# A new emission order and PSUM pools from tables, in a kernel of linear attention and an MLP

## The chip, the core and the metric

One core of a Trainium2 chip. The metric is the device time of one execution, in microseconds (us). Engines are called by the profile's names: PE is the TensorE matmul, PEld its weight load, DVE VectorE, ACT ScalarE, POOL GpSimd, SP the engine whose queue issues the DMAs.

## The reference

Attention with random features, then an MLP, all in float32. Batch 8, 8 heads, 576 tokens, head width 64, 128 features; the MLP has 4608 tokens, model width 512, inner width 2048.

```python
q_s, k_s = q * scale, k * scale                  # scale = 64 ** -0.25
def phi(x):
    h = einsum('bhsd,md->bhsm', x, omega) - sum(x * x) / 2
    return exp(h - max(h)) / sqrt(m)
kv = einsum('bhsm,bhsd->bhmd', phi(k_s), v);  z = sum(phi(k_s), axis=2)
attn = einsum(phi(q_s), kv) / (einsum(phi(q_s), z) + 1e-6)
x = attn as (4608, 512);  h = x @ w_in
out = (h * sigmoid(h)) @ w_out
```

## The kernel before, in words

**Windows.** Attention works in 32 windows, one for each batch and pair of heads. A window n goes through a chain over all engines: SP loads q, k and v (raw, nat, v). PE projects them on omega (proj for k and for q; mid or mids for the middle block; in windows 18 to 31 one proj unit does k and q). DVE takes the row maxima (top, nb). ACT does the exp (exp in strips of four blocks of columns, or DVE subtracts and ACT does expall). POOL adds the columns of phi(k) (sums, esl; ACT does esh between them). PE spreads that sum to all rows (z, line 664). DVE computes the denominators against it (den, line 696). POOL multiplies phi(q) by their reciprocals (norm, line 707; DVE in three windows). PE transposes the result in three triples (turn, line 713), ACT copies each out of PSUM (en, line 717). PE computes phi(k) times v (kv, line 672), ACT copies it (kt), PE transposes it (ktt, line 680), ACT copies it (kw), and PE multiplies for the numerator (num, line 734). From window 2 on, kv of window n + 1 and num of window n are one unit, kvnum. ACT copies the result (xh), and for the first 12 windows DVE makes a low half (xl). In windows 0 to 7 the squares are done by ACT on the raw input (r2, line 546).

**The MLP.** Four windows are one tile of 512 tokens. Every float32 operand is split into a high and a low part, so that each product is three fp32r matmuls of 128x512 (`thrice`, line 905). Tile 0 runs stage 1 (units s1, three matmuls each) and stage 2 (s2) in full. Its weights are taken from the input, rounded and split by ACT (re, wh), DVE (wd) and POOL (wlo). Tiles 1 to 8 go by pairs with seven products of sums of quarters in place of eight: tiles 1 and 2 run stage 1 in full, then `pr` units (six matmuls) for stage 2; the later pairs run `deep` units for stage 1, too. ACT applies Silu (silu, sA, si) and makes high parts (hi, ohi), DVE makes differences and low parts (dif, lo, xd, olo).

**The order of the work.** All this is registered as 3716 units in `Plan` (line 122): 933 for PE, 863 for ACT, 960 for DVE, 423 for POOL, 537 for SP. A unit has an engine, a duration in the plan, a function that emits its instructions, the units it needs, the ring buffers it takes and frees, and the number of PSUM banks it takes. `Plan.run` (line 139) is a list scheduler in the kernel's Python code: at each step it takes, over the engines, the ready unit that could start first by its own durations, ties within 0.25 us going to the lower number in the table `RANK` (line 282). Line 1546 then emits the units in that order. Each engine's queue runs its instructions in the order in which they are emitted, so the order of an engine is fixed when the kernel is built. In this kernel the numbers in `RANK` are the places, 0 to 3715, in which the scheduler issues the units: it reproduces its table unit for unit.

**PSUM.** There are eight banks in three pools: acc (4) for stage 2 and the sums of products, h (2) for stage 1 of tiles 0 to 2, att (2). A bank that an attention unit takes comes from the pool that `bank_pools` (inside `Plan.run`, line 171) chooses: always att, and h or acc too in stretches in which its rules allow it. A unit waits for the last reader of the buffer that it is given. ACT must load another function table (`ACT_TABLE_LOAD`) whenever it changes between exp and Silu.

Of the kernel before, what the change touches and what calls it, by code (L numbers as in the profile page):

```python
# [21 lines left out]
NPAIR = H // 2  # L22
# [12 lines left out]
LAG = 2  # L35
# [40 lines left out]
SWITCH = 1.3  # L76
HANDOFF = {"PE": 0.3, "ACT": 0.25, "DVE": 0.22, "POOL": 0.2, "SP": 0.2}
CALM = 0.5
TURN = 0.14
# [36 lines left out]
def tiled_by(u):  # L116
    if u["name"][0] == "proj" and u["name"][1] in FOLD:
        return None
    return {"proj": "rows", "kv": "columns", "num": "columns", "kvnum": "columns"}.get(u["name"][0])


class Plan:
# [16 lines left out]
    def run(self):  # L139
        assert len(RANK) == len(self.units)  # L140
        rank = dict(zip(self.units, RANK))
        end, first = {}, {}
        slots = {r: [] for r in RINGS}
        pipe = port = 0.0
        holds = []
        free_at = {e: 0.0 for e in ("PE", "ACT", "DVE", "POOL", "SP")}
        table = mode = None
        order = []
        children, missing = {}, {}
        ready = {e: [] for e in free_at}  # L150
        for n, u in self.units.items():
            missing[n] = len(u["after"]) + len(u["order"])
            for a in u["after"] + u["order"]:
                children.setdefault(a, []).append(n)
            if not missing[n]:
                ready[u["eng"]].append(u)

        freed = {r: [] for r in RINGS}
        home, frees, users = {}, {}, {}
        for x, names in self.freed_by.items():  # L160
            users[x] = len(names)
            for n in names:
                frees.setdefault(n, []).append(x)

        def slot_time(ring, back=0):
            i = len(slots[ring]) + back - RINGS[ring]
            if i < 0:
                return 0.0
            return freed[ring][i] if i < len(freed[ring]) else None

        def bank_pools(u):
            pools = ["att"]
            if u["key"] > mm_time(START[2] + MIX):
                pools.append("h")
            if u["key"] < mm_time(24 * LAG) - 1 or (
                LEND[0] < u["key"] < LEND[1] and slots["acc"] and slots["acc"][-1][0] != "ch"
            ):
                pools.append("acc")
            if u["key"] < START_MLP - 1:
                pools.append("h")  # L180
            chosen, when, used = [], 0.0, {p: 0 for p in pools}
            for _ in range(u["banks"]):
                best = None
                for p in pools:
                    t = slot_time(p, used[p])
                    if t is not None and (best is None or t < best[0]):
                        best = (t, p)
                if best is None:
                    return None, None
                used[best[1]] += 1  # L190
                chosen.append(best[1])
                when = max(when, best[0])
            return chosen, when

        while any(ready.values()):
            best = None
            for e, us in ready.items():
                pick, least = None, None
                for u in us:
                    t = 0.0  # L200
                    for a in u["after"]:
                        if self.units[a]["eng"] == e and not self.units[a]["lat"]:
                            t = max(t, end[a])
                        else:
                            t = max(t, first[a] + (CALM if e == "PE" and t > START_MLP else 0.0))
                    ok, taken = True, []
                    for ring, _ in u["alloc"]:
                        s = slot_time(ring, taken.count(ring))
                        taken.append(ring)
                        if s is None:  # L210
                            ok = False
                            break
                        t = max(t, s)
                    pools = ()
                    if ok and u["banks"]:
                        pools, s = bank_pools(u)
                        ok = pools is not None
                        if ok:
                            t = max(t, s)
                    if not ok:  # L220
                        continue
                    t = max(t, free_at[e])
                    if u["port"] and e == "POOL":
                        t = max(t, port)
                    elif u["port"]:
                        for a, b in holds:
                            if a <= t < b:
                                t = b
                    key = rank[u["name"]]
                    least = t if least is None else min(least, t)  # L230
                    pick = (pick or []) + [(u, pools, key, t)]
                if not pick:
                    continue
                p = min((p for p in pick if p[3] <= least + 0.25), key=lambda p: p[2:])
                if best is None or p[3] < best[3]:
                    best = p
            assert best is not None, [u["name"] for us in ready.values() for u in us][:40]
            u, pools, _, t = best
            e, n = u["eng"], u["name"]
            ready[e].remove(u)  # L240
            dur = u["dur"]
            if u["table"] and u["table"] != table:
                dur += SWITCH
                table = u["table"]
            if e == "PE":
                if tiled_by(u) != mode:
                    dur += TURN
                mode = tiled_by(u)
            u["cost"] = dur
            free_at[e] = t + dur  # L250
            if u["port"] and e == "POOL":
                n_ = int(u["port"])
                holds = holds[-12:] + [(t + dur * i / n_, t + dur * (i + 1) / n_ - 0.05) for i in range(n_)]
            elif u["port"]:
                port = t + dur
            done = t + dur
            if u["lat"]:
                pipe = max(pipe, t + dur + 1.0) + u["lat"]
                done = max(pipe, t + dur + 2.2) + LANDING
            end[n] = done  # L260
            first[n] = done + HANDOFF[e]
            for ring, i in u["alloc"]:
                slots[ring].append(i)
                home[i] = ring
            for j, p in enumerate(pools):
                slots[p].append(("bank", n, j))
                home["bank", n, j] = p
            for x in frees.get(n, ()):
                users[x] -= 1
                if not users[x]:  # L270
                    freed[home[x]].append(max(end[a] + HANDOFF[self.units[a]["eng"]] for a in self.freed_by[x]))
# [1336 lines left out]
```

## Time and profile before

| | |
|---|---|
| median of 3 runs | 982.38 us (982.08 to 982.41) |
| the profiled execution's own time | 978.92 us |
| its span, first to last instruction | 977.1 us |
| mean granted TensorE clock | 0.994 |
| busy PE / DVE / ACT / POOL | 948.6 / 764.9 / 646.5 / 402.7 us |

The span is what the profile's rows divide up. The profiled execution is 3.46 us shorter than the median of the runs; its own time lies 1.8 us over the span. The busy time of PE counts overlapping matmuls once, and a stall of a fraction of a matmul inside a stream does not show as idle.

### The profile page before, as it was taken

How to read it: one execution, taken by the hardware profiler on the slowest of the kernel's cores; microseconds unless marked ns; L12 is line 12 of the kernel's file. 1: busy time of each engine (PE TensorE's matmuls, PEld its weight loads, DVE VectorE, ACT ScalarE, POOL GpSimd, SP SyncE). 2: the span in 40 equal slices, each digit the busy share in tenths (PEclk: the TensorE clock that was granted, in tenths of full speed). 3: DMA queues.
4: the chain of work that ended last, by engine and by line, in shares of the span. 5: the costliest groups of instructions: out<-in, count | busy, mean ns of one | idle time of the engine just before them, and what ended most of it. 6: DMA issues, size and time to landing. Idle time of an engine off the chain costs nothing.

```text
span 977.1 us, 16378 instructions
## 1 busy us (share of the span) xinstructions
PE 948.6 (97%) x5558; PEld 767.2 (79%) x5558; DVE 764.9 (78%) x1610; ACT 646.5 (66%) x1233; POOL 402.7 (41%) x430
## 2 busy tenths in 40 slices
PE   7879999999999999997999999999999999999998
PEld 6667887787787778785778888778888887888886
DVE  4778998588764988757999999669799966369954
ACT  8999787687987675697478766665384544235442
POOL 3666555868775858547631444222012220000000
PEclk9899999999999999999999999999999999999999
DMA  8388997999987698886676666676554556556562
GB/s 240 112 273 286 311 363 268 328 371 307 307 299 267 223 336 301 301 285 229 215 274 223 206 239 222 216 241 206 182 194 174 185 205 226 192 189 221 192 214 103
DMA packets 102708, 237.61 MB, mean 243 GB/s; under 512 B 13664, under 2 KB 44512, under 8 KB 102624
## 3 DMA queue, kind: packets, MB, share of 16 engines
q1 hardware_dynamic: 102480, 236.49, 71.3%
q8 instruction: 45, 0.74, 0.3%
q14 instruction: 39, 0.32, 0.1%
q10 hardware_dynamic: 144, 0.07, 0.0%
HBM read 192.48 MB, written 44.04 MB: 242 GB/s over the span
## 4 chain that ended last, share of the span: by engine, by line
PE 80%; ACT 9%; DVE 8%; issue 1%; DMA 1%; POOL 0%; DVEq 0%; ACTq 0%; POOLq 0%
PE ps_acc L905 56%; PE ps_h L905 9%; PE ps_att L558 3%; PE ps_att L672 2%; ACT hk L613 2%; PE ps_att L713 2%; PE ps_h L558 1%; ACT hq L613 1%; ACT in L546 1%; PE ps_att L734 1%; DVE prod L696 1%; PE ps_h L734 1%; PE ps_h L713 1%; ACT g L787 1%; DVE g L997 1%
## 5 line engine op out<-in xcount | busy, mean ns | idle before, releaser
L905 PE MATMUL ps_acc<-ts,w 128*128 128x512 f32 x2544 | 612.1, 394 | 4.3 <-ACT ts L916 1.4
L905 PEld LDWEIGHTS ps_acc<-ts,w 128*128 128x128 f32 x2544 | 469.1, 188 | 104.2 <-ACT ts L916 1.9
L947 ACT CAST ts<-g 128x1024 fp32r<-128x1024 f32 x112 | 118.0, 1055 | 118.5 <-PE ps_acc L905 114.5
L951 DVE TENSOR_TENSOR ts<-g,ts 128x1024 fp32r<-128x1024 f32 x112 | 143.7, 1287 | 33.1 <-ACT ts L947 32.9
L905 PE MATMUL ps_h<-xq,w 128*128 128x512 f32 x576 | 149.6, 400 | 0.1
L707 POOL TENSOR_TENSOR hq<-hq,rd 128x384 f32<-128x384 f32 x87 | 90.3, 1060 | 93.9 <-DVE rd L702 84.2
L905 PEld LDWEIGHTS ps_h<-xq,w 128*128 128x128 f32 x576 | 103.8, 188 | 21.6 <-DVE xq L760 0.4
L997 DVE TENSOR_TENSOR g<-ps_acc,g 128x512 f32<-128x512 f32 x144 | 95.6, 685 | 26.0 <-PE ps_acc L905 24.8
L642 POOL TENSOR_TENSOR t<-hk 128x256 f32<-128x256 f32 x64 | 55.4, 882 | 121.2 <-ACT hk L634 62.7
L943 DVE TENSOR_TENSOR g<-g,g 128x1024 f32<-128x1024 f32 x64 | 88.1, 1390 | 5.1 <-ACT g L938 4.6
L819 POOL TENSOR_TENSOR w<-g,w 128x512 fp32r<-128x512 f32 x32 | 44.9, 1417 | 31.9 <-ACT w L815 15.7
L655 POOL TENSOR_TENSOR es<-t,es 128x256 fp32r<-128x256 f32 x32 | 28.2, 882 | 60.9 <-ACT es L651 60.8
L1001 ACT ACTIVATE g<-g 128x1024 f32<-128x1024 f32 x36 | 37.7, 1059 | 22.9 <-DVE g L997 22.8
L696 DVE CUSTOM_DVE_ANT_0 prod<-hq,ps_att 128x128 f32<-128x128 f32 (+1 forms) x150 | 42.9, 286 | 11.6 <-PE ps_att L664 6.8
L542 DVE TENSOR_REDUCE sq<-in 128x9 f32<-128x576 f32 x48 | 34.8, 744 | 20.0 <-ACT in L537 19.5
L647 POOL TENSOR_TENSOR t<-t,hk 64x128 f32<-64x128 f32 x64 | 37.4, 584 | 23.7 <-ACT hk L613 20.0
L963 ACT CAST ts<-xq 128x1024 fp32r<-128x1024 f32 x21 | 22.2, 1057 | 37.2 <-PE ps_acc L905 36.8
L967 DVE TENSOR_TENSOR ts<-xq,ts 128x1024 fp32r<-128x1024 f32 x21 | 26.1, 1244 | 22.2 <-ACT ts L963 22.2
L696 DVE CUSTOM_DVE_ANT_0 prod<-hq,ps_h 128x128 f32<-128x128 f32 (+1 forms) x120 | 34.3, 286 | 6.1 <-PE ps_h L664 1.9
L1024 DVE TENSOR_TENSOR c<-ps_acc,c 128x512 f32<-128x512 f32 x48 | 30.8, 682 | 7.6 <-PE ps_acc L905 7.6
L862 POOL TENSOR_TENSOR ic<-ic 128x512 f32<-128x512 f32 x16 | 24.3, 1519 | 28.2 <-DMA ic<-w_d 15.9
L613 ACT ACTIVATE hk<-ps_att,nbk 128x128 f32<-128x128 f32 x117 | 33.9, 397 | 2.6 <-DVE nbk L592 2.2
(172 smaller groups left out, 1443.0 us busy)
## 6 DMA issues: line engine op xcount, KB each, us to landing
w<-w_d SPq DMA_DIRECT2D x168, 512.0 KB, 4.2
w<-ws_d SPq DMA_DIRECT2D x48, 512.0 KB, 4.0
v<-v SPq DMA_DIRECT2D x32, 320.0 KB, 5.0
out<-c SPq DMA_DIRECT2D x17, 512.0 KB, 4.4
in<-kT SPq DMA_DIRECT2D x24, 352.0 KB, 3.9
in<-qT SPq DMA_DIRECT2D x24, 352.0 KB, 5.3
g<-w_in SPq DMA_DIRECT2D x16, 512.0 KB, 5.1
g<-w_out SPq DMA_DIRECT2D x16, 512.0 KB, 6.0
```

Of the source, the lines that this page charges most:

```text
L558: nc.tensor.matmul(ps[:, cols], T["raw", n, who][r, o : o + P], oms[r], start=True, stop=True)
L613: nc.scalar.activation(h[:, c], ps[:, i * M : (i + 1) * M], AF.Exp, bias=bias_of(n, who, c), scale=-1.0 if n in FOLD else 1.0)
L642: nc.gpsimd.tensor_tensor(t[:, i], e[:, 5 * i : 5 * i + 2], e[:, 5 * i + 2 : 5 * i + 4], ALU.add)
L696: nc.vector.tensor_tensor_reduce(out=prod[r], in0=e[r, c], in1=z[r, j * M : (j + 1) * M], scale=1.0, scalar=GUARD, op0=ALU.mult, op1=ALU.a ...
L707: nc.gpsimd.tensor_tensor(e[:, c], e[:, c], rd[:, c].unsqueeze(2).broadcast_to([P, 3, M]), ALU.mult)
L819: nc.gpsimd.tensor_tensor(lo, T["w", i], hi.bitcast(F32), ALU.subtract)
L905: nc.tensor.matmul(ps, w(a), x[:, b], start=first and n == 0, stop=last and n == 2, **more)
L943: nc.vector.tensor_tensor(out, a, b, ALU.subtract)
L947: nc.scalar.copy(g[:, 0], T["g", p, SOURCE[j], u])
L951: nc.vector.tensor_tensor(g[:, 1], T["g", p, SOURCE[j], u], g[:, 0].bitcast(F32), ALU.subtract)
L997: nc.vector.tensor_tensor(to, T["q", p, chain, i], T["g", p, r, i // 2][:, i % 2], ALU.add)
L1001: nc.scalar.activation(g, g, AF.Silu)
```

## The change

The scheduler goes. The kernel emits the units sorted by a new table `RANK` of the same length, and the pool of each attention bank is read from a string `HOMES`, one letter for each of the 395 banks. Units, functions, instructions, ring sizes and dependencies are the same. The durations in the `add` calls change too, and two tables MODES and CHANGE are added, but nothing in the emitted program depends on them any more.

```diff
     def run(self):
         assert len(RANK) == len(self.units)
-        rank = dict(zip(self.units, RANK))
...
-        def bank_pools(u):
-            pools = ["att"]
-            if u["key"] > mm_time(START[2] + MIX):
-                pools.append("h")
...
-                p = min((p for p in pick if p[3] <= least + 0.25), key=lambda p: p[2:])
...
-        return order
+        order = sorted(zip(RANK, self.units.values()), key=lambda x: x[0])
+        homes, done = iter(HOMES), set()
+        for _, u in order:
+            assert done.issuperset(u["after"]) and done.issuperset(u["order"]), u["name"]
+            done.add(u["name"])
+            u["pools"] = [{"a": "att", "c": "acc", "h": "h"}[next(homes)] for _ in range(u["banks"])]
+        return [u for _, u in order]
 
 RANK = (
-    0, 1, 13, 2, 11, 15, 17, 19, 22, 23, 3, 14, 18, 25, 29, 30, 27, 24, 33, 31, 37, 42, 49, 6, 40, 41, 43, 47, 48, 51,
...
+)
+HOMES = (
+    "achacchaaccchcchcaacchahcacchaahcccachchccachhcchhachhacchacaahcacaccaahhahaaaaahahahaaahahaaahaahaa"
...
-        add(zn, "PE", 0.24, at(n, 7, 32), lambda ps, n=n: zsum(n, ps), after=[("esl", n)] + e["q"], banks=1,
+        add(zn, "PE", 0.233, at(n, 7, 32), lambda ps, n=n: zsum(n, ps), after=[("esl", n)] + e["q"], banks=1,
...
```

Counted from the two tables, the least number of units that must be moved to turn one order into the other: PE 272, ACT 468, DVE 433, POOL 124, SP 228. The banks of attention come from att, h and acc 213, 115 and 67 times before, 154, 129 and 112 times after; 204 of the 395 differ. "PE work" between two places of PE's order is, in what follows, the sum of the shortest spacings of the units between them in the trace (0.68 us for an s1 or s2 unit, 1.36 for pr and deep, 2.2 for kvnum, 1.9 for a proj of both, 1.7 for a proj of windows 0 to 7, 0.24 for a turn).

PE's order of the opening, from the proj of window 3 (a number alone is a window; [s1 x4] stands for four s1 units):

```
before: proj3k num0 z1 proj2q mid2q mid3k turn1 turn1 z2 turn1 proj3q kvnum1 mid3q proj4k ktt2 turn2 turn2 mid4k
        turn2 [s1 x2] z3 proj4q mid4q kvnum2 turn3 ktt3 turn3 proj5k mid5k [s1] turn3 kvnum3 proj5q ktt4 z4 mid5q
        [s1 x5] [s2 x3] turn4 [s1 x4] proj6k [s2 x4] ...
after:  proj3k z1 turn0 turn0 turn0 ktt0 proj2q mid2q ktt1 num0 turn1 mid3k turn1 z2 turn1 proj3q mid3q kvnum1
        proj4k mid4k turn2 ktt2 z3 turn2 turn2 proj4q kvnum2 mid4q proj5k mid5k turn3 turn3 turn3 ktt3 proj5q
        kvnum3 z4 [s1 x3] mid5q [s1] ktt4 [s1 x4] proj6k [s1 x3] turn4 [s1] [s2 x4] ...
```

Ahead of its first Silu, ACT had r2 of window 6 (q) and 7 (k), two re passes, kw of window 4 and the last strip of exp of window 5 (q); after the change these stand behind it, and the short xh copy of window 2 stands ahead.

PE's order around the proj of window 20 (D is a deep unit):

```
before: D kvnum17 turn18 x3 ktt18 proj20 D D D mids20 z19 kvnum18 ktt19 turn19 x3 z20 kvnum19 ktt20 proj21 D D
after:  D z18 kvnum17 D proj20 D turn18 x3 mids20 z19 D ktt18 D kvnum18 turn19 ktt19 turn19 x2 z20 kvnum19 D proj21
        ktt20 D D
```

The z unit of window 19 takes a bank of pool h in both. Before, it is the one that the second q strip of exp of window 20 frees; after, the one that a k strip of the same window frees.

## Rows read from the trace of the kernel before

**Rows 1.** Stretches: length; busy (count) of PE, PEld, DVE, ACT, POOL; clock; DMA; GB/s.
```profile
10.20:34.00 23.80, 19.17 (x172) 16.85 (x171) 15.01 (x61) 22.66 (x69) 13.20 (x20) 1.00 0.59 177
34.00:41.00 7.00, 4.88 (x21) 4.28 (x22) 5.35 (x20) 6.90 (x18) 6.62 (x9) 0.51 0.49 130
41.00:72.00 31.00, 26.78 (x216) 21.39 (x214) 25.29 (x84) 30.61 (x80) 20.07 (x25) 1.00 0.76 241
...
250.00:436.00 186.00, 185.94 (x1141) 148.82 (x1141) 136.05 (x281) 141.47 (x296) 125.02 (x120) 1.00 0.84 287
436.00:484.00 48.00, 42.05 (x305) 32.08 (x305) 38.14 (x103) 31.27 (x84) 32.96 (x38) 0.96 0.63 214
```

**Rows 2.** Timeline of ACT, 57 to 72 us (start, length, instruction, [idle before]).
```profile
57.56 1.16 ACT L546 ACTIVATE in<-in 64x1152 f32<-64x1152 f32 x1
...
63.70 1.36 ACT L787 ACTIVATE g<-g 128x512 f32<-128x512 f32 x2
...
66.53 0.68 ACT L787 ACTIVATE g<-g 128x512 f32<-128x512 f32 x1 [0.20 <-DMA g<-w_out]
...
68.83 1.13 ACT L613 ACTIVATE hq<-ps_att,nbq 128x128 f32<-128x128 f32 x4
69.98 1.28 ACT L916 ACT_TABLE_LOAD   x1
71.27 0.60 ACT L916 ACTIVATE ts<-ps_h 128x512 fp32r<-128x512 f32 x1
```

**Rows 3.** Timeline of PE in the opening.
```profile
35.79 0.90 PE L713 MATMUL ps_acc<-ident,hq 128*128 128x128 f32 x3 [3.94 <-POOL hq L707]
...
71.92 0.50 PE L905 MATMUL ps_acc<-ts,w 128*128 128x512 f32 x1 [1.44 <-ACT ts L916]
73.13 2.13 PE L905 MATMUL ps_acc<-ts,w 128*128 128x512 f32 x8 [0.71 <-DVE ts L921]
75.11 0.49 PE L713 MATMUL ps_att<-ident,hq 128*128 128x128 f32 x3
75.35 3.00 PE L905 MATMUL ps_h<-xq,w 128*128 128x512 f32 x12
78.19 1.95 PE L554 MATMUL ps_att<-omn,in 128*128 128x128 f32 x16
```

**Rows 4.** Timeline of PE, 439 to 468 us.
```profile
439.17 1.31 PE L672 MATMUL ps_att<-hk,v 128*64 128x128 f32 x20
...
441.38 0.55 PE L713 MATMUL ps_h<-ident,hq 128*128 128x128 f32 x3
441.77 0.49 PE L713 MATMUL ps_att<-ident,hq 128*128 128x128 f32 x3
...
453.72 0.62 PE L664 MATMUL ps_h<-es,ones 128*128 128x256 f32 x2 [1.35 <-ACT hq L613]
454.75 2.40 PE L672 MATMUL ps_att<-hk,v 128*64 128x128 f32 x20 [0.41 <-ACT hk L613]
...
459.79 0.55 PE L713 MATMUL ps_h<-ident,hq 128*128 128x128 f32 x3 [0.69 <-POOL hq L707]
...
467.74 4.48 PE L905 MATMUL ps_acc<-ts,w 128*128 128x512 f32 x17
```

**Rows 5.** Timeline of PE, 303 to 308 us.
```profile
303.09 1.52 PE L905 MATMUL ps_acc<-ts,w 128*128 128x512 f32 x6
304.54 1.16 PE L558 MATMUL ps_att<-oms,in 64*128 64x128 f32 x16
...
306.44 1.53 PE L905 MATMUL ps_acc<-ts,w 128*128 128x512 f32 x6
307.81 0.39 PE L905 MATMUL ps_h<-xq,w 128*128 128x512 f32 x1
```

**Rows 6.** Group of ACT's transpose copies by form (busy us, mean ns of one, idle before).
```profile
L717 ACT COPY en<-ps_att 128x384 f32<-128x384 f32 x52 | 24.4, 489 | 12.3 <-PE ps_att L713 11.9
```

**Rows 7.** DMA issues of the page (count, KB each, median us to landing).
```profile
w<-w_d SPq DMA_DIRECT2D x168, 512.0 KB, 4.2
```

More of the change, by code (lines that the diff above doesn't have):

```diff
@@ L113, with mode_of @@
 LEND = (mm_time(TILE0 + 12), mm_time(START[2]) - 8)
-def tiled_by(u):
+MODES = {
+    "proj": "rows", "kv": "columns", "num": "columns", "kvnum": "columns", "turn": "turned", "ktt": "turned",
+    "mid": "full", "mids": "full", "z": "few",
+}
+CHANGE = {
+    "rows": {None: 0.235, "columns": 0.33, "turned": 0.16, "full": 0.2, "few": 0.21},
+    "columns": {None: 0.13, "rows": 0.22, "turned": 0.06, "full": 0.1, "few": 0.11},
+    "turned": {None: 0.11, "rows": 0.2, "columns": 0.2, "turned": 0.08, "full": 0.11, "few": 0.14},
+    "full": {None: 0.097, "rows": 0.19, "columns": 0.19, "turned": 0.08, "full": 0.08, "few": 0.09},
+    "few": {None: 0.026, "rows": 0.12, "columns": 0.12, "turned": 0.02, "full": 0.02},
+    None: {"rows": 0.09, "columns": 0.09, "turned": 0.006},
+}
+def mode_of(u):
     if u["name"][0] == "proj" and u["name"][1] in FOLD:
-        return None
-    return {"proj": "rows", "kv": "columns", "num": "columns", "kvnum": "columns"}.get(u["name"][0])
+        return "full"
+    return MODES.get(u["name"][0])
 class Plan:
@@ L140, in run @@
         assert len(RANK) == len(self.units)
-        rank = dict(zip(self.units, RANK))
[L142 to L169, printed above, removed]
-        def bank_pools(u):
-            pools = ["att"]
-            if u["key"] > mm_time(START[2] + MIX):
-                pools.append("h")
[L175 to L233, printed above, removed]
-                p = min((p for p in pick if p[3] <= least + 0.25), key=lambda p: p[2:])
[L235 to L271, printed above, removed]
-            u["pools"], u["at"] = list(pools), t
-            order.append(u)
-            for c in children.get(n, ()):
-                missing[c] -= 1
-                if not missing[c]:
-                    ready[self.units[c]["eng"]].append(self.units[c])
@@ L278, in run @@
-        assert len(order) == len(self.units), [n for n in self.units if n not in end][:20]
-        return order
-RANK = (
[186 rows of a table removed]
+        order = sorted(zip(RANK, self.units.values()), key=lambda x: x[0])
[5 more added lines that the diff above has]
+        return [u for _, u in order]
@@ L1049, in bk @@
         return ("bank", name, j)
-    add("warm", "PE", 1.4, -9, warm, banks=1, free=[bk("warm")])
+    add("warm", "PE", 2.4, -9, warm, banks=1, free=[bk("warm")])
     add("load_omega", "ACT", 0.4, -9, load_omega, lat=0.1)
```

32 lines of the change are left out of this document (17 added, 15 removed), and 371 rows, old and new, of the table RANK.

## The prediction

> **What bounds the kernel now.** I read first the page, then the busy time by stretch, then each engine's timeline where a stretch stood out. The table of stretches [rows 1] splits the run in three kinds. From 250 to 436 us TensorE (PE) is busy 185.94 of 186 us: such a stretch can only get shorter if its own instructions do, and these don't change. The opening is different: from 10.2 to 72 us ScalarE (ACT) is busy 22.66 of 23.8, 6.90 of 7 and 30.61 of 31 us, while PE is idle for 4.63, 2.12 and 4.22 us and for 7 us of it has a granted clock of 0.51. So the opening is bound by ACT's queue, and it lasts as long as the work that ACT does before PE has enough to go on. The third kind is the stretch from 436 to 484 us, where PE is idle for 5.95 of 48 us and neither ACT (31.27) nor VectorE (38.14) is full: a chain of waits. Two places are thus open to another order, worth at most some 20 us; the rest is open only to harm.
>
> **The opening.** Before the first Silu at 71.27 [rows 2] ACT does, in the old order, work that the new order puts behind that Silu: the square at 57.56 (1.16), one of the two exponent passes at 63.70 (half of 1.36), and all that it issues from 66.53 to 68.83 (the other exponent pass, a copy, a square, one exp strip; 2.30). That is 4.1 us; one short copy comes forward, and I take 4.0. If ACT stays as full as it is, the first Silu starts 4.0 us earlier. PE meanwhile waits 1.44 us for that Silu at 71.92 and 0.71 us at 73.13 for the low half that follows it [rows 3]. In the new order three things stand ahead of that first stage-2 product that stood behind it: the transpose triple at 75.11, the 12 products at 75.35 (to 78.19, so 2.84) and the projection at 78.19, 5 us of PE work in all. They can cover both waits, 2.1 us. Upper end: 4.0 + 2.1 = 6.1 us. Lower end: ACT has to wait as much as it was spared, nothing gained; that it loses more is the business of a rival. I take 4.5, nearer the upper end, because ACT is already full in the old order and because the tables give the chains there more room: between a window's column-sum product (z) and its first transposes, the denominators and the normalizing must fit. Counted in TensorE work, windows 0, 1 and 3 had 2.9, 2.0 and 4.1 us there and get 3.8, 3.8 and 6.4. The 3.94 us idle before the transposes at 35.79 [rows 3] are such a wait of window 1.
>
> **The stretch from 436 us.** Its PE rows [rows 4] show the z product of window 19 waiting 1.35 us at 453.72 for ACT's exp of window 20, since both its candidate banks hold window 20's projections. Behind it VectorE's denominators, then GpSimd's normalizing, then the transposes at 459.79 (0.69 of wait) and the numerator, and only then the operand of the product at 467.74. The twenty matmuls of kv take 1.31 us at 439.17 and 2.40 at 454.75, where the engine had just waited at 453.72: the clock fell, and its mean of 0.96 over the stretch [rows 1] is 0.04 × 48 = 1.9 us of full speed lost. Open are 5.95 + 1.9 = 7.85 us. In the new order the projections of window 20 go out one product unit earlier, the z of window 19 stands ahead of three product units that were ahead of it, it takes a bank that an earlier strip of exp frees, and two products, a transpose and kv-numerator (5.0 us) lie between it and its transposes where 2.2 us lay. The chain from z to the transposes takes 459.79 − 453.72 = 6.07 us, of which 5.0 are now covered. One wait for z itself (exp of window 20, about 1.3 as now) stays, and some of the last step. I take 6.0 gained, with 0 and 7.85 as ends.
>
> **Regrouping.** The stream of PE changes between the products of the MLP and attention 337 times in the old order and 209 times in the new. That looks like a gain, but pairs of neighbouring attention units rise as much, outside these two stretches from 54 to 116. Entering a projection out of six products costs 304.54 − 303.09 = 1.45 against 307.81 − 306.44 = 1.37, so 0.08 [rows 5]; a transpose triple behind another takes 441.77 − 441.38 = 0.39 [rows 4] against 0.24 in front of a product (75.11 to 75.35) [rows 3], so 0.15 more. 64 entries less at 0.08 are −5 us, 62 neighbours more at 0 to 0.15 are +0 to +9. I take 0, ends −3 and +4.
>
> **Banks.** Of 395 banks that attention takes, 204 change their pool: the two pools that the MLP's own products use lend 112 and 129 instead of 67 and 115. In the old order every product that opens a bank for the MLP stands at least 2.3 us of PE work behind the unit after which that bank can be freed; in the new one 13 have less than 1.5, 11 of them behind a copy of attention's, mostly of transposes (en). Such a copy takes 0.49 us [rows 6]; if ACT is free, the spacing is enough, if ACT is in an exp strip or a table load of 1.28 [rows 2], PE waits up to about 1.3 us. 13 times 0 to 1.3 is 0 to 17 us. ACT has idle time there (busy 141.47 of 186 [rows 1], so three times in four it is in something, mostly of half a microsecond). I take 0.15 each, 2 us.
>
> **Moves that cost nothing.** ACT changes between exp and Silu 55 times instead of 65; ten loads of 1.28 [rows 2] go, 12.8 us of ACT, none before the first Silu, all beside products that bind; without that cover they would count whole. The load at 69.98 delays ACT by no more than itself: the Silu starts at 71.27, 1.29 us later. The Trainium skill ("ScalarE: Activation LUTs", section "What ACT_TABLE_LOAD costs") puts a switch at some 2.66 us with a drain, by which 26.6 us would leave ACT; the row shows half of that. SP's queue is reordered at 228 of 537 units; for a weight load the least PE work between the moment its issue can start and its first product rises from 5.1 to 8.1 us, over the landing time of 4.2 [rows 7], so no product waits for a load; with less than 4.2 each would cost the difference. GpSimd's 124 moved units are sums and normalizing, counted in the chains above. The planner itself ran on the host.
>
> **Sum.** −4.5 − 6.0 + 0 + 2.0 = −8.5 us. The profiled execution took 978.92 (span 977.1), so 970.4 in its like; the median of the runs is 3.46 higher, 982.38, and by the same difference I forecast **973.9**.
>
> **Rivals.**
> *The opening doesn't shorten* (ACT, which serves its queue in order, meets as many waits as it was spared). For it: the new order takes window 0's last copies 7 us of ACT work later. Against: these aren't needed until the first products. Then −6.0 + 2.0: 978.4. Chance 0.15.
> *The clock drops in the opening.* From 34 to 41 us PE's clock is at 0.51, the 1.2 GHz level, after the idle 3.94 us before 35.79 [rows 1, 3]; PE was busy 4.88 us of it, half of which full clock would save, 2.4 us. The new order puts the first MLP products 11 us of PE work later, so fewer fill the early gaps; two more such drops are +4.9: −3.6, 978.8. Chance 0.05. The Trainium skill ("TensorE: Matmul & The Clock Gate", section "HAM oscillation — how this bites in real kernels") warns that idle gaps in TensorE's stream throttle it; the trace agrees where it fell.
> *Slower: the lent banks.* The 13 close places wait the whole 1.3 us, 17 us in place of 2: +6.5, 988.9. It decides from 0.8 us a place on. For it: these waits didn't exist before, and ACT's copy stands in line. Against: ACT's load falls by 12.8 us. Chance 0.13.
> *No change.* Gains and new waits cancel, 982.4: 0.09. That the two tables differ in nothing that counts is excluded by the counts above.
>
> **How the numbers follow.** The forecast has 0.58. Its ends: 4.0 + 2.1 + 7.85 + 3 = 17.0 down, 965.5, with no new wait; up, to 983.5, the range takes in the first two rivals and no change. Left out are the lent banks (0.13) and a little below. A measurement of this kernel can tell about 0.2%, 2 us. Faster: 0.58 + 0.15 + 0.05 = 0.78; within 0.2%: 0.09; slower: 0.13.
>
> **What would show it.** In the changed profile: the first Silu near 67 us in place of 71.27; PE's idle from 10 to 86 us less by some 4 us; the z product of window 19 without 1.35 us of wait, the product of 467.74 some 10 us earlier, of which 4 from the opening; the granted clock near 1.00 throughout; 56 table loads (66 before); new short waits of products for L717. Wrong it would be if ACT has idle time before the first Silu, if products wait for L717 by over 10 us in sum, or if PE's idle moves to another stretch.

## The result, and the profile after

The changed kernel takes 967.81 us (median of 4 runs, 964.88 to 968.51) against 982.23 us for the kernel before: a ratio of 0.9849 (95% interval 0.9828 to 0.987), 14.4 us less. The forecast of 973.9 us had the sign and the range right and was 6.1 us too slow. The profiled execution took 964.88 us, 14.0 less than that of before.

In the changed kernel all lines below `Plan` have numbers lower by 113: L713 of the transposes is now L600, L905 of the products L792, L664 of z L551. The stretches, in the columns of [rows 1], read in the profile after:

```profile
10.20:34.00 23.80, 19.41 (x173) 16.68 (x173) 17.38 (x64) 23.22 (x77) 16.25 (x24) 1.00 0.61 185
34.00:41.00 7.00, 5.76 (x40) 5.20 (x41) 5.81 (x25) 6.90 (x14) 3.06 (x4) 0.76 0.10 35
41.00:72.00 31.00, 29.27 (x226) 24.04 (x223) 27.06 (x80) 30.13 (x82) 24.81 (x28) 1.00 0.71 220
250.00:436.00 186.00, 184.93 (x1141) 149.47 (x1137) 135.97 (x291) 131.97 (x285) 124.90 (x124) 1.00 0.85 299
436.00:484.00 48.00, 44.56 (x309) 34.21 (x308) 43.03 (x123) 32.32 (x93) 29.21 (x36) 1.00 0.64 222
```

PE's idle time in the first three stretches fell from 10.97 to 7.36 us, in the last one from 5.95 to 3.44, and the clock of that last stretch is 1.00 in place of 0.96. That is 6.1 us of idle time, less than half of the gain. From 250 to 436 us it rose, from 0.06 to 1.07, so a little idle time came up elsewhere; over the whole span it fell by 5.2 us. The rest of the gain is not in any idle time. The first line of the page, of the kernel before and then of the changed one:

```profile
PE 948.6 (97%) x5558; PEld 767.2 (79%) x5558; DVE 764.9 (78%) x1610; ACT 646.5 (66%) x1233; POOL 402.7 (41%) x430
```
```profile
PE 939.8 (98%) x5558; PEld 766.0 (80%) x5558; DVE 760.7 (79%) x1610; ACT 630.7 (65%) x1223; POOL 392.6 (41%) x430
```

The same 5558 matmuls keep PE busy 8.8 us less. A part of that is the granted clock, which was 0.51 and 0.96 in two of the stretches and is 0.76 and 1.00 there now; in the long stretches it is 1.00 in both. And PE's two costliest groups, before and after (columns: operations, busy us, mean ns, idle before):

```profile
L905 PE MATMUL ps_acc<-ts,w 128*128 128x512 f32 x2544 | 612.1, 394 | 4.3 <-ACT ts L916 1.4 <-DVE ts L921 0.9 <-DVE ts L967 0.9
L905 PE MATMUL ps_h<-xq,w 128*128 128x512 f32 x576 | 149.6, 400 | 0.1
```
```profile
L792 PE MATMUL ps_acc<-ts,w 128*128 128x512 f32 x2544 | 601.7, 392 | 0.9 <-DVE g L884 0.4 <-issue 0.3
L792 PE MATMUL ps_h<-xq,w 128*128 128x512 f32 x576 | 142.4, 395 | 0.4 <-DVE hk L517 0.2
```

A product's mean time falls by 2 and 5 ns with nothing changed in it. To see where the time lies one must look below the idle time: for every PE unit I take the spacing from its first matmul to the next unit's first matmul, less the shortest such spacing of its kind in the kernel before (the "PE work" of the section on the change), and add these up. I call that sum the loss. In us, by stretches of PE work, so that the same work stands in one row:

| PE work | before | after | gain |
|---|---|---|---|
| 0 to 60 us, the opening | 30.2 | 25.7 | 4.5 |
| 60 to 390 us | 19.9 | 17.3 | 2.6 |
| 390 to 420 us, windows 18 to 20 | 13.1 | 8.0 | 5.1 |
| 420 us to the end | 12.9 | 10.6 | 2.3 |
| sum | 76.1 | 61.6 | 14.5 |

In the second and the last row, the steady stretches, PE goes from products to attention 157 times before and 90 times after. Spacings with an excess of up to 0.25 us add up to 28.6 us before and 24.6 after; the longer ones, real waits, to 4.2 (10 of them) and 3.3 (5). So 4.0 of these 4.9 us were in excesses too short to show as idle time. From the timeline of PE after, one can read them:

```profile
321.25 1.52 PE L792 MATMUL ps_acc<-ts,w 128*128 128x512 f32 x6
...
336.03 1.66 PE L792 MATMUL ps_acc<-ts,w 128*128 128x512 f32 x6
...
431.20 1.66 PE L792 MATMUL ps_acc<-ts,w 128*128 128x512 f32 x6
```

Six products behind other products take 1.52 us, as in [rows 5]; six behind an attention unit 1.66. The first matmul of nearly every return takes 0.1 us longer, and the engine counts as busy in it. The exception is a return from a column-sum product z. In 19 of the 21 returns from z in the trace after, the second matmul starts 0.22 to 0.24 us behind the first, as inside a product; in all 84 returns from other attention units it starts 0.31 to 0.34 us behind it, and so it does in the two behind a z that had itself waited for over 1 us (441.21 below is one).

The two other stretches look as forecast, with one exception. The timelines of ACT and of PE after:

```profile
64.21 1.17 ACT L433 ACTIVATE in<-in 64x1152 f32<-64x1152 f32 x1
65.40 0.21 ACT L643 COPY xr<-ps_acc 128x64 f32<-128x64 f32 x1
65.63 1.28 ACT L803 ACT_TABLE_LOAD   x1
66.92 0.60 ACT L803 ACTIVATE ts<-ps_h 128x512 fp32r<-128x512 f32 x1
```
```profile
440.84 0.50 PE L551 MATMUL ps_h<-es,ones 128*128 128x256 f32 x2 [1.40 <-ACT hk L500]
441.21 1.66 PE L792 MATMUL ps_acc<-ts,w 128*128 128x512 f32 x6
442.70 0.27 PE L567 MATMUL ps_att<-ident,kt 128*128 128x128 f32 x1
442.88 1.65 PE L792 MATMUL ps_acc<-ts,w 128*128 128x512 f32 x6
444.46 1.31 PE L559 MATMUL ps_att<-hk,v 128*64 128x128 f32 x20
...
446.68 0.55 PE L600 MATMUL ps_acc<-ident,hq 128*128 128x128 f32 x3
...
455.04 4.72 PE L792 MATMUL ps_acc<-ts,w 128*128 128x512 f32 x18
```

The first Silu starts at 66.92 us (71.27 in [rows 2]). The z of window 19 still waits, 1.40 us, now for a k strip of window 20; but its transposes at 446.68 wait for nothing, the kv matmuls run at full clock (1.31 us; 2.40 in [rows 4]), and the product of 467.74 in [rows 4] starts at 455.04. No product waits for a transpose copy by over 0.3 us.

### The profile page after: what moved, and what is told of

It is laid out like the page before. It is cut to its first block, busy times and chain, and to the rows that moved or that the text cites. A ratio compares the mean times of both kernels' runs of the same rounds, so it can differ in the third digit from the quotient of the medians.

```text
span 963.1 us, 16285 instructions
## 1 busy us (share of the span) xinstructions
PE 939.8 (98%) x5558; PEld 766.0 (80%) x5558; DVE 760.7 (79%) x1610; ACT 630.7 (65%) x1223; POOL 392.6 (41%) x430
## 4 chain that ended last, share of the span: by engine, by line
PE 85%; ACT 6%; DVE 5%; DMA 2%; issue 1%; POOL 1%; DVEq 0%; POOLq 0%; ACTq 0%; SPq 0%
PE ps_acc L792 57%; PE ps_h L792 12%; PE ps_acc L445 2%; PE ps_att L621 1%; PE ps_att L445 1%; PE ps_att L559 1%; ACT hk L500 1%; ACT hq L500 1%; PE ps_h L559 1%; PE ps_h L445 1%; PE ps_att L600 1%; DMA in<-kS 1%; DVE prod L583 1%; PE ps_h L600 1%; DMA g<-w_in 1%
## 5 line engine op out<-in xcount | busy, mean ns | idle before, releaser
L792 PE MATMUL ps_acc<-ts,w 128*128 128x512 f32 x2544 | 601.7, 392 | 0.9 <-DVE g L884 0.4
L792 PEld LDWEIGHTS ps_acc<-ts,w 128*128 128x128 f32 x2544 | 472.1, 188 | 98.7 <-issue 0.7
L792 PE MATMUL ps_h<-xq,w 128*128 128x512 f32 x576 | 142.4, 395 | 0.4 <-DVE hk L517 0.2
L792 PEld LDWEIGHTS ps_h<-xq,w 128*128 128x128 f32 x576 | 105.9, 188 | 23.7 <-ACT kw L572 0.6
L594 POOL TENSOR_TENSOR hq<-hq,rd 128x384 f32<-128x384 f32 x87 | 86.7, 1017 | 62.2 <-DVE rd L589 54.2
L884 DVE TENSOR_TENSOR g<-ps_acc,g 128x512 f32<-128x512 f32 x144 | 94.3, 684 | 18.3 <-PE ps_acc L792 17.0
L529 POOL TENSOR_TENSOR t<-hk 128x256 f32<-128x256 f32 x64 | 50.0, 797 | 107.9 <-ACT hk L500 65.2
L830 DVE TENSOR_TENSOR g<-g,g 128x1024 f32<-128x1024 f32 x64 | 83.9, 1333 | 1.5 <-ACT g L825 1.3
L583 DVE CUSTOM_DVE_ANT_0 prod<-hq,ps_h 128x128 f32<-128x128 f32 (+1 forms) x150 | 42.9, 286 | 14.6 <-PE ps_h L551 9.6
L583 DVE CUSTOM_DVE_ANT_0 prod<-hq,ps_att 128x128 f32<-128x128 f32 (+1 forms) x140 | 40.0, 286 | 14.2 <-PE ps_att L551 9.4
L888 ACT ACTIVATE g<-g 128x1024 f32<-128x1024 f32 x36 | 38.0, 1062 | 17.4 <-DVE g L884 17.3
L424 ACT ACTIVATE in<-in 128x576 f32<-128x576 f32 x48 | 33.5, 704 | 2.6 <-DMA in<-kn 2.6
L749 POOL TENSOR_TENSOR ic<-ic 128x512 f32<-128x512 f32 x16 | 25.7, 1613 | 21.9 <-DMA ic<-w_d 21.7
```

What stands on the lines that cost most here:

```text
L529: nc.gpsimd.tensor_tensor(t[:, i], e[:, 5 * i : 5 * i + 2], e[:, 5 * i + 2 : 5 * i + 4], ALU.add)
L583: nc.vector.tensor_tensor_reduce(out=prod[r], in0=e[r, c], in1=z[r, j * M : (j + 1) * M], scale=1.0, scalar=GUARD, op0=ALU.mult, op1=ALU.a ...
L594: nc.gpsimd.tensor_tensor(e[:, c], e[:, c], rd[:, c].unsqueeze(2).broadcast_to([P, 3, M]), ALU.mult)
L792: nc.tensor.matmul(ps, w(a), x[:, b], start=first and n == 0, stop=last and n == 2, **more)
L830: nc.vector.tensor_tensor(out, a, b, ALU.subtract)
L884: nc.vector.tensor_tensor(to, T["q", p, chain, i], T["g", p, r, i // 2][:, i % 2], ALU.add)
```

## The experiments

All times of this section are medians; each ratio is to the kernel before, run beside it. "Order" in the diffs is the order of one engine's queue.

**1. The old opening alone.**

```diff
 RANK, HOMES:
-all 3716 units in the new order, new pools
+units 0 to 447 of the old order with their old pools, then all others in the new order, new pools
```

> The first 448 units are emitted in the old order with their old PSUM pools (TensorE work of about the first 95 us), all others in the new order with the new pools. Theory (the opening's gain is its own and reaches the end, since TensorE bounds everything behind it): the profile of this kernel shows TensorE's idle time from 10 to 72 us as before the change (4.63, 2.12 and 4.22 us in its three parts), a first Silu near 71.3 us, and the whole run is 4.6 us slower than the changed kernel, 972.4 us (ratio to the kernel before 0.990). Rival 1 (the opening's gain is given back later, by waits that the old opening does not have): the run stays within 1 us of the changed kernel, 968. Rival 2 (the new order needs its own opening, because windows are further behind in the old one): over 976.

Measured: 972.07 us (0.9896, interval 0.9877 to 0.9915). The stretches:

```profile
10.20:34.00 23.80, 19.49 (x173) 17.18 (x171) 14.85 (x59) 22.36 (x68) 13.20 (x20) 1.00 0.59 176
34.00:41.00 7.00, 4.56 (x20) 3.96 (x21) 5.47 (x21) 6.88 (x19) 6.30 (x8) 0.55 0.54 144
41.00:72.00 31.00, 27.04 (x216) 21.73 (x215) 25.33 (x86) 29.79 (x78) 20.06 (x26) 0.99 0.74 229
```

PE's idle time of [rows 1] is back (4.31, 2.44 and 3.96 us), the first Silu starts at 72.43, and the loss behind the opening is the changed kernel's to a few tenths, but for 0.7 in the stretch of windows 18 to 20. So the opening's gain is its own and reaches the end: 4.3 us by the medians, 5.7 against the second set of runs of the changed kernel (experiment 7).

**2 and 3. More switching, and the same at other places.** Only PE's queue is changed, in the steady stretches; a piece of it in each of the two kernels (s1(1,14,2) is a stage-1 unit of tile 1):

```diff
-s1(1,14,2) s1(1,14,3) z11 s1(1,15,0) s1(1,15,1) s1(1,15,2) s1(1,15,3) kvnum10 proj13k
+s1(1,14,2) s1(1,14,3) s1(1,15,0) z11 s1(1,15,1) kvnum10 s1(1,15,2) s1(1,15,3) proj13k
```
```diff
-s1(1,8,3) s1(1,9,0) z9 s1(1,9,1) s1(1,9,2) s1(1,9,3) turn8 x3 ... s1(1,10,1) s1(1,10,2) proj11k turn9 x3
+s1(1,8,3) turn8 s1(1,9,0) z9 s1(1,9,1) s1(1,9,2) s1(1,9,3) turn8 x2 ... s1(1,10,1) turn9 s1(1,10,2) proj11k turn9 x2
```

> Only TensorE's queue is changed, and only outside the opening and the stretch around window 20: product units are moved so that the stream goes from products to attention 153 times instead of 104 (168 in the kernel before); every other queue, the pools and the 56 table loads are those of the changed kernel. Theory (switching costs: entering and leaving attention are paid on every excursion, and neighbours inside an excursion cost less): in the two traces the steady stretches lose 32.8 and 27.9 us beyond the shortest spacings, with 157 and 90 entries, so 0.074 us for each entry less; 49 more make 3.6 us, 971.4 us (ratio 0.989), spread over the run, without idle time of over 0.3 us at any one place. Rival, the forecast's own term (regrouping worth nothing, because neighbours cost what entries save; the steady stretches gained by shorter waits of the other queues): 967.8 us, within 1 us of the changed kernel.

> As the kernel with more alternation, but the product units are moved to other places, where what they wait for has long been done; entries from products into attention 153 in the whole run, 104 in the changed kernel; all other queues and the pools as in the changed kernel. Theory (each excursion into attention has a price of its own, 3.5 us for 49 in the first such kernel, and the rest of its loss, 4.2 us, was in five or so waits of 0.6 to 1.3 us that the moves made by chance): the spacings with under 0.25 us of excess again lose some 3.5 us more than in the changed kernel, the longer waits under 1.5 us more, and the run takes 971.5 us (ratio 0.989). Rival (the waits were the cause, the price is not one of switching): the loss goes with the long waits, and the run is within 1 us of the changed kernel, 967.8 us.

Measured: 973.33 us (0.9907, 0.9889 to 0.9925) and 971.26 us (0.9896, 0.9878 to 0.9915). The loss of the steady stretches, and the entries into attention there:

| | before | after | first | second |
|---|---|---|---|---|
| entries | 157 | 90 | 139 | 139 |
| short excesses, us | 28.6 | 24.6 | 28.1 | 28.0 |
| longer waits, us (count) | 4.2 (10) | 3.3 (5) | 7.5 (10) | 4.2 (5) |

Both put 49 entries more than the changed kernel and lose 3.5 and 3.4 us more in short excesses: 0.07 us an entry, where the change itself saved 4.0 us on 67 entries, 0.06 each. The first kernel's expectation missed that its moves also made waits of 0.6 to 1.3 us; with other places they are gone, and the price stays. Switching is what the steady stretches gained by. The price is one of putting such excursions in or taking them out; the bare number of entries does not give the loss of another order (experiment 8).

**4. z of window 19 behind two products, as in the old order.**

```diff
-turn18 x3 mids20 z19 D ktt18 D kvnum18 turn19 ktt19
+turn18 x3 mids20 D ktt18 D z19 kvnum18 turn19 ktt19
```

> The changed kernel with one unit moved: the column-sum product z of window 19 stands behind the two product units that the change put behind it, as in the old order. Theory (the chain from z over denominators and normalizing to the transposes takes 6.07 us and needs products beside it): z's own wait of 1.65 us goes, but the first transposes of window 19 wait for GpSimd's normalizing by some 3 to 5 us, net 3 us slower, 970.8 us (ratio 0.988). Rival (what the new order bought here is only z's earlier bank, and z waits in any case): 1.65 us faster, 966.2 us, no wait at the transposes.

Measured: 970.75 us (0.9881, 0.9862 to 0.99). PE's timeline:

```profile
442.15 2.92 PE L792 MATMUL ps_acc<-ts,w 128*128 128x512 f32 x6 [1.76 <-ACT en L604]
...
446.72 0.40 PE L551 MATMUL ps_h<-es,ones 128*128 128x256 f32 x2
...
451.74 0.55 PE L600 MATMUL ps_acc<-ident,hq 128*128 128x128 f32 x3 [2.40 <-POOL hq L594]
...
454.57 1.91 PE L559 MATMUL ps_h<-hk,v 128*64 128x128 f32 x20
```

z waits for nothing, but the transposes wait 2.40 us for GpSimd's normalizing, six products take 2.92 us and the kv matmuls 1.91: the clock fell after these waits, as in [rows 4] (0.93 granted from 436 to 484 us, 1.00 in the changed kernel). The loss of this stretch is 12.9 us against 8.0 after and 13.1 before. By this count the one place is worth nearly all that the stretch gained; by the medians it is worth 2.9 us, 4.4 against the second set of runs of the changed kernel. What I had not expected is the wait at 442.15: with z gone from between, the first product needs a bank that the copy of the transposes (en) frees. So not all of the 4.9 us is the chain behind z. By the spacings, the wait for the bank comes in place of z's own (2.0 us for 1.65), the product behind it loses 1.2 us more at the low clock, and 2.5 us are the wait of the transposes.

**5 and 6. ScalarE's work ahead of the first Silu.** First in the changed kernel (ACT's queue), then in the kernel with the old opening:

```diff
-... r2(6,k) xh3 silu0 silu8 re_in9 exp5q ... re_out9 ... r2(6,q)
+... r2(6,k) xh3 r2(6,q) re_in9 re_out9 silu0 silu8 exp5q ...
```
```diff
-kw3 r2(6,q) exp4q ... silu0 re_in2 xh2 silu8 exp5q
+kw3 exp4q ... silu0 re_in2 xh2 silu8 r2(6,q) exp5q
```

> The changed kernel with three units of ScalarE moved back ahead of the first Silu, where they stood in the old order: the square of window 6 (q), 1.16 us, and two exponent passes, 0.68 us each; 2.5 us in all. TensorE's order is the new one. Theory (the opening lasts as long as ScalarE's queue ahead of the first Silu): the first Silu starts 2.5 us later, at 69.4 instead of 66.9 us, the first stage-2 product waits, and the run is 2 us slower, 969.8 us (ratio 0.987). Rival (the opening was shortened by TensorE's order, with products that cover the wait for the Silu): the first Silu starts 2.5 us later, but no product waits for it; within 0.5 us of the changed kernel, 967.8 us.

> The kernel with the old opening, and in it one unit of ScalarE moved: the square of window 6 (q), 1.16 us, goes from its old place behind the second Silu of stage 1. Theory, the forecast's own step (ScalarE's queue ahead of the first Silu is full, so what is taken out of it brings the Silu forward by as much): the first Silu starts 1.2 us earlier than in the kernel with the old opening (72.43 us there), the wait of the first stage-2 product for it (2.27 us there) shrinks to 1.1, and the run is 1.2 us faster, 970.9 us. Rival (in the old order of TensorE the queue of ScalarE waits elsewhere for as long, for a transposed triple or a load): the first Silu moves by under 0.4 us and the run stays at 972.1 us or gets longer by up to 1.

Measured: 968.58 us (0.9861, 0.9841 to 0.9881) and 972.98 us (0.9911, 0.9893 to 0.993). In the first the Silu starts at 69.89 us, 2.97 later, and PE's timeline has

```profile
71.75 3.88 PE L792 MATMUL ps_h<-xq,w 128*128 128x512 f32 x9 [2.22 <-DVE ts L808]
```

It is a stage-1 product that waits, for a bank that VectorE's low half behind the Silu frees, and not a stage-2 product. The loss of the opening is 28.2 us against 25.7, of the rest the same; but five profiles with the changed kernel's opening (its own, and those of experiments 2, 3, 4 and 7) have 25.7 to 27.1 there, the medians differ by 0.8 us only, by 2.2 against the second set of runs, and the changed kernel's own runs span 3.6. So it costs between 1 and 2.5 us, and theory and rival are not told apart: a Silu that is 2.97 us later costs less than that. In the second, ACT's timeline:

```profile
65.35 0.22 ACT L643 COPY xr<-ps_acc 128x64 f32<-128x64 f32 x1
67.10 0.67 ACT L674 ACTIVATE g<-g 128x512 f32<-128x512 f32 x1 [1.53 <-DMA g<-w_out]
67.67 0.25 ACT L572 COPY kw<-ps_acc 128x128 f32<-128x128 f32 x1
67.93 1.17 ACT L433 ACTIVATE in<-in 64x1152 f32<-64x1152 f32 x1
...
71.83 0.60 ACT L803 ACTIVATE ts<-ps_h 128x512 fp32r<-128x512 f32 x1
```

The 1.16 us taken out gave 0.6 at the Silu: ACT now waits 1.53 us for the load of w_out (0.20 in [rows 2], 1.03 in the kernel with the old opening), and PE, earlier by more than the Silu is, waits 2.77 us for it (2.27 there). The rival holds, though the Silu moved by somewhat more than it allowed. In the old order work taken from ACT's queue becomes a wait for a DMA, because an exponent pass that needs this load still stands ahead of the Silu; the new order puts that pass behind.

**7 and 8. The changed kernel again, and a third order.** The third moves, against the changed kernel, 207 units of PE, 415 of ACT, 410 of DVE, 110 of POOL and 214 of SP, and 193 pools. A piece of PE's order:

```diff
-z9 s1(1,9,1) s1(1,9,2) s1(1,9,3) turn8 x3 mids10 proj10q kvnum8 s1(1,10,0) s1(1,10,1) s1(1,10,2) proj11k turn9 x3
+mids10 z9 s1(1,8,0) ... s1(1,9,1) kvnum8 turn9 s1(1,9,2) s1(1,9,3) proj10q proj11k turn9 x2 s1(1,10,0)
```

> The changed kernel itself, beside the next one on the same chip: 967.8 us, ratio 0.985. Its steady stretches show the same 24.6 us of short excess as in its first profile, since they hang on the order alone; the opening may differ by about 1 us.

> A third order of the same units, built from the changed kernel's by moving single units and changing pools where its trace still shows waits: the z of window 5 (1.57 us at 81.0), the last transposes of window 18 (1.31 at 436.9), the transposes of window 9 (0.98 at 216.2) and z of window 16 (0.72 at 373.3). Entries from products into attention 115 (104 in the changed kernel), table loads 64 (56). Theory (TensorE bounds everything behind the opening, so each of these waits that goes is gained whole, 11 entries at 0.06 to 0.07 us cost 0.7): 4.6 less what stays of them, about a third, less 0.7, so 2.5 us faster than the changed kernel, 965.3 us (ratio 0.9825). Rival (the waits move to other units, and eight more table loads of 1.28 us make ScalarE late): 967.8 us or slower.

Measured: 966.36 us (0.9843, 0.9824 to 0.9862) and 984.47 us (1.0025, 1.0012 to 1.0039). The second profile of the changed kernel has 24.1 us of short excesses in the steady stretches (24.6 in the first) and 4.2 us of longer waits in 7 places (3.3 in 5), so two profiles of one kernel differ by 0.5 and 0.9 us here. The third order, for which I expected 965.3, is 18 us slower than the changed kernel and slower than the one before, though its short excesses are the smallest so far (23.7 us in the steady stretches, with 11 entries more than in the changed kernel). Its longer waits there are 21.4 us in 22 places. The longest, on PE, and the queues of DVE and POOL at that time:

```profile
143.89 1.52 PE L792 MATMUL ps_acc<-ts,w 128*128 128x512 f32 x6
149.41 1.62 PE L792 MATMUL ps_h<-xq,w 128*128 128x512 f32 x3 [4.00 <-DVE ts L808]
```
```profile
139.34 0.67 DVE L688 SCALAR_TENSOR_TENSOR g<-g,g 128x512 uint32<-128x512 uint32 x1
...
146.94 1.72 DVE L688 SCALAR_TENSOR_TENSOR g<-g,g 128x512 uint32<-128x512 uint32 x1
148.59 0.68 DVE L808 TENSOR_TENSOR ts<-ps_h,ts 128x512 fp32r<-128x512 f32 x1
```

```profile
139.50 1.12 POOL L531 TENSOR_TENSOR t<-t 128x256 f32<-128x256 f32 x1
...
145.46 1.01 POOL L594 TENSOR_TENSOR hq<-hq,rd 128x384 f32<-128x384 f32 x1
146.43 0.90 POOL L534 TENSOR_TENSOR t<-t,hk 64x128 f32<-64x128 f32 x1
147.29 0.82 POOL L594 TENSOR_TENSOR hq<-hq,rd 128x384 f32<-128x384 f32 x1
```

The low half that the product needs (148.59) stands behind passes over weights for later, and one of these, of the same shape, takes 0.67 us at 139.34 and 1.72 at 146.94, beside GpSimd's normalizing and column sums (the third fence, GpSimd's queue). These two rows alone do not show that GpSimd is the reason, since it is busy beside the first of them too (139.50). All rows together bear it out. In the 13 profiles of this case, VectorE's passes of L688 and L692 (128x512, operands in SBUF alone; L801 and L805 in the kernel before) that meet no GpSimd instruction take 0.67 to 0.70 us, all 392 of them; those with GpSimd at work for over 95% of their time take 0.67 to 1.81, 117 of 144 of them over 0.72. VectorE's operations with an operand in PSUM (L808 and L884; L921 and L997 before) take 0.63 to 0.69 us beside GpSimd, all 360. In the eighth kernel 17 of the 64 passes of L688 and L692 meet no GpSimd instruction, in the changed kernel 29.

**9 to 11. Orders that keep something.** The next two again move units of all queues (139 of PE, 373 of ACT, 375 of DVE, 82 of POOL, 218 of SP; and 143, 367, 397, 81, 212), the last one 84 of PE and 79 pools alone:

```diff
 ninth:
-s1(1,8,3) s1(1,9,0) z9 s1(1,9,1) s1(1,9,2) s1(1,9,3) turn8 x3 mids10 proj10q kvnum8
+s1(1,8,3) turn8 x2 ktt8 turn8 s1(1,9,0) z9 mids10 s1(1,9,1) s1(1,9,2) proj10q s1(1,9,3) kvnum8
 tenth:
-s1(1,8,3) s1(1,9,0) z9 s1(1,9,1) s1(1,9,2) s1(1,9,3) turn8 x3 mids10 proj10q kvnum8
+s1(1,8,3) turn8 x2 s1(1,9,0) z9 turn8 s1(1,9,1) mids10 s1(1,9,2) s1(1,9,3) proj10q s1(1,10,0) kvnum8
 eleventh (PE and pools alone):
-s1(1,8,0) s1(1,8,1) s1(1,8,2) s1(1,8,3) s1(1,9,0) z9 s1(1,9,1) s1(1,9,2) s1(1,9,3) turn8 x3
+s1(1,8,0) turn8 x2 s1(1,8,1) s1(1,8,2) s1(1,8,3) s1(1,9,0) z9 s1(1,9,1) s1(1,9,2) turn8 s1(1,9,3)
```

> Again a third order built from the changed kernel's, with the same aim as the last one, but with one thing kept that the last one gave up: VectorE's operations on SBUF operands and GpSimd's are ordered so that they seldom fall together. Entries from products into attention 115, table loads 58. In the last kernel VectorE was busy 776.2 us and GpSimd 408.7 for the same instructions that took 760.7 and 392.6 in the changed kernel, and TensorE waited 6.0 us for VectorE's low halves. Theory (these collisions were the loss): VectorE stays at 760 us or less, GpSimd at 390 or less, no wait of TensorE for VectorE over 0.5 us, and the run is 2 to 4 us faster than the changed kernel, 964 us (ratio 0.982). Rival (any other order lets chains come late that the changed one has in step): 970 us or slower, with VectorE's busy time as in the changed kernel.

> A second order with the same aim, found from the changed kernel by other moves; table loads 54. Theory as for the one before: 964 us, VectorE at 760 us or less. If the two differ by over 3 us, something that neither the price of switching nor the collisions cover decides.

> From the changed kernel, 84 of TensorE's 933 units are moved and the pools of 79 attention banks changed, again towards fewer waits and no more switching (entries 108, the changed kernel 104); the queues of ScalarE, VectorE, GpSimd and SyncE are the changed kernel's, unit for unit. Theory (what the three further orders lost came from their reordering of the other queues, in which VectorE was 9 to 16 us busier): VectorE is back at 762 us or less, no stretch behind the opening is more than 1 us worse than in the changed kernel, and the run takes 965 to 968 us (ratio 0.983 to 0.986). Rival (TensorE's order and the pools did it): waits in the middle of the steady stretches as in the two further orders before, 969 us or slower.

Measured: 968.41 us (0.9867, 0.9852 to 0.9881), 974.62 us (0.9938, 0.9917 to 0.9958) and 965.57 us (0.9831, 0.9812 to 0.985). The first lines of their pages:

```profile
PE 942.0 (97%) x5558; PEld 767.4 (79%) x5558; DVE 775.7 (80%) x1610; ACT 632.3 (65%) x1225; POOL 404.1 (42%) x430
```
```profile
PE 943.8 (97%) x5558; PEld 769.6 (79%) x5558; DVE 769.8 (79%) x1610; ACT 626.1 (64%) x1221; POOL 398.3 (41%) x430
```
```profile
PE 943.4 (98%) x5558; PEld 770.0 (80%) x5558; DVE 762.7 (79%) x1610; ACT 631.0 (65%) x1223; POOL 393.5 (41%) x430
```

The ninth was to keep VectorE at 760 us, at 964 us in all, and did neither: VectorE is as busy as in the eighth (776.2), yet the run is 16 us shorter. So the longer operations alone are not the loss; they cost where PE waits for what stands behind them, 6.0 us for low halves in the eighth, nowhere over 0.8 us behind the start in the ninth. The tenth differs from the ninth by 6 us, which neither the price of switching (102 and 100 entries in the steady stretches) nor VectorE's total explains: two waits make most of it, 2.5 us at transposes and 2.2 at z, both for results of VectorE. With the other queues left as they were, in the eleventh, VectorE is back at 762.7 and the run at 965.57, as expected, which cannot be told from the changed kernel's 966.36. What exactly makes the waits of the eighth and the tenth stays open. That they came from reordering the other queues is likely, not shown: the eleventh has another order of PE than they have, with fewer moves, and the ninth reordered the other queues as much as the tenth and lost 2 us, not 8.

## Why the prediction was right, and where its sum was off

The forecast's terms were −4.5, −6.0, 0 and +2.0. The loss gives −4.5 for the opening, −5.1 for the stretch, −4.0 for the short excesses of the steady stretches and −0.9 for their longer waits. So the sum was 6 us short: 4.0 in regrouping and 2.9 in the banks, less 0.9 that the stretch gave too little. The range held the result because its lower end took every gain in full.

- **The opening** (−4.5) was right in size: −4.5 by the loss, which differs by up to 1.4 us between profiles of the same opening, and the run with the old opening is 4.3 to 5.7 us slower by its median. The Silu came 4.35 us earlier (forecast 4.0), and the first stage-2 products do not wait for it. That an earlier Silu is worth as much at the end is not shown: in experiment 4 it is 2.97 us later and the run 0.8 to 2.2 us longer, so a part of the gain is PE's new order. The reason needs a correction: "if ACT stays as full as it is" holds only because the exponent pass that waits for w_out goes behind the Silu too. Experiment 6 took out one square and got a DMA wait for it.
- **The stretch from 436 us** (−6.0) gave −5.1, and mostly for the reason named: products lie between z and its transposes. Moved back alone, z costs 4.9 us of loss there, of which 2.5 are the wait of the transposes; the rest is the wait for a bank and the lower clock. The list of signs had z without its wait; the working had said that one wait would stay, and that was right (1.40 us).
- **Regrouping** is the step that failed: "I take 0, ends −3 and +4". It came to −4.0, outside these ends. I priced the entry (0.08) and the neighbour (0 to 0.15) and left out the return: a spacing from a transpose to the first product looked like the cheapest way out (75.11 to 75.35 in [rows 3]), but the price lies inside the product unit, in its first matmul. Six products show it, 1.66 us for 1.52. Sorted by the unit in which it lies, the short excess of product units, which holds entries and returns, fell by 8.0 us (22.1 to 14.1), where I had 5 for the entries alone; that of attention units, which holds the neighbours, rose by 4.1 (6.4 to 10.5), inside my 0 to 9. Experiments 2 and 3 put entries back and pay 0.07 us each, net of neighbours.
- **The lent banks** (+2.0, up to 17) cost next to nothing. Behind the opening, the largest excess in front of a product that waits for one of ScalarE's copies, the 13 close places included, is 0.36 us in the trace after (a deep unit at 456.8, behind a kw copy); most show the 0.1 us that nearly any return costs. The longer waits of the steady stretches, these places included, went from 4.2 to 3.3 us, and to 4.2 in the second profile of the changed kernel, so they did not rise. The rival on the other side had its place right and its price wrong: ACT came in time.
- **The claim ahead of the terms**, that a stretch with PE busy 185.94 of 186 us "can only get shorter if its own instructions do", was wrong. From 484 to 823 us PE is idle for 0.25 us of 339 before and for none after, and of the work from 420 us on 2.3 us of loss went all the same.
- **Table loads** went from 66 to 56 and ACT's busy time from 646.5 to 630.7 us, beside products, as forecast. The clock did not drop more often: between 10 and 72 us only the stretch from 34 to 41 is low, 0.76 where it was 0.51. The rivals of no shortening and of a dropping clock both fall.

Of what changed, experiment 1 shows the opening, 4 the place of z, 2 and 3 the switching. By the ratios, each taken beside the kernel before, experiments 1, 4 and 3 are 4.6, 3.1 and 4.6 us slower than the changed kernel, each to within some 3 us; their sum, 12.3, is near the whole 14.4, but they were not taken back together, and experiment 3 put back 49 of 67 entries. The 0.9 us of longer waits was not tried by itself and is no more than two profiles of one kernel differ by.

The Trainium skill has a rule that bears on the switching ("TensorEngine Tiling (Array Packing)", section "Tiling Modes"): changing the tiling mode, not just the tile, drains TensorE. The trace agrees for the entry: projections of the later windows (64x128 tiles) and kv (128x64) have a median excess of 0.09 us in front of them behind products (128x128), transposes, z and middle blocks, all 128x128, 0.03 or less. For the return it does not suffice: products are 0.1 us late behind transposes too, and behind z, also 128x128, they are mostly not. What makes the return cost stays open.

## What to carry to other kernels

An engine that is busy all the time can still lose time: compare the spacing of the same work in two kernels, not the busy share, and price a switch between kinds of matmul on both sides, at the entry and in the first matmul after the return. What a short chain needs is work of the bound engine between its steps; one unit at the wrong place cost 3 to 5 us here. And an order must be judged on all queues: one with less switching loss on PE was 18 us slower, with PE waiting for results that stood late in VectorE's queue.

## What the runs showed of the hardware that I had not expected

The first product after attention, most returns from z excepted, takes 0.1 us longer and counts as busy; 67 such excursions less were worth 4.0 us. VectorE's passes over SBUF operands alone took 0.67 to 0.70 us away from GpSimd's work and up to 1.81 beside it, for one shape, while those with an operand in PSUM stayed at 0.69 or less. In the third order VectorE was busy 776.2 us and GpSimd 408.7 with the instructions that take 760.7 and 392.6 in the changed kernel. The Trainium skill ("GPSIMD Engine Reference", section "1. Specifications") says that GpSimd shares its SBUF interfaces with VectorE and contends with VectorE instructions that run in a 2-port perf mode or have two SBUF inputs. The rows agree: the passes of L688 and L692 have two inputs in SBUF and slow down, those with one input in PSUM do not, and both engines grew together, by 15.5 and 16.1 us, without an operation added.
